# Q tails as rows of two tokens, x of two batches turned by DMA, turned q of one batch on VectorE, the last tile in halves, and a new order of every engine: a change to a scheduled attention-and-mixer kernel

## The chip, the cores, the metric

One core of one Trainium2 chip. The metric is device time in microseconds (us) of one execution. The kernel before took 213.88 us (median of six runs: five of 213.44 to 215.09 and one outlier of 687.24, its first execution). Engines: PE is TensorE (matmul), PEld its weight load, DVE is VectorE, ACT is ScalarE, POOL is GpSimd, SP is SyncE, whose only work here is to issue DMA transfers. PSUM is the memory that TensorE writes its results to.

## The reference

```
kv  = einsum('bhsd,bhse->bhde', k, v)            # 8 batches, 8 heads, 576 tokens, 64 wide
x   = einsum('bhsd,bhde->bhse', q, kv)           # then divided by its rms, times g_norm
x   = x, heads side by side                      # [8, 576, 512]
th  = x @ w_theta
y   = w_tok_r @ (x*cos(th)) + w_tok_i @ (x*sin(th))   # mixes tokens, 576 x 576
u   = x + y
out = u + relu(u @ w_ch)
```

576 tokens are four tiles of 128 and a tail of 64. Everything on TensorE is in f16 but the k/v product (f32).

## The kernel before

The kernel holds a list scheduler of its own. A function lists some 1,200 operations with engine, estimated duration, dependences and buffers; a greedy pass places each on its engine by tables of priorities (found by an earlier search) and emits each engine's instructions in that order. **Each engine then runs its list strictly in order**: an instruction that waits holds up everything behind it on its engine. The plan also gives a start time for each operation, so a trace can be compared with it; "late by 3 us" below means 3 us after the planned start. (The plan is the kernel's own estimate, no time of the chip.)

The parts that matter, cut (a cut is marked `# ...`):

```python
CAPS = {"raw": 3, "raw0": 1, "th": 5, ...}   # PSUM banks by use; raw0: products of batch 0's pairs

def load_ql(b):                              # the q tail: 64 tokens on 64 partitions, 256 B pieces
    nc.sync.dma_start(out=live["qls", b][0:T], in_=q[b, :, SF:S, :].rearrange("h s d -> s h d"))

def cast_ql(b, r):                           # two casts of 64 partitions
    (nc.gpsimd if b else nc.vector).tensor_copy(live["qcs", b][0:T, NF]..., live["qls", b][0:T]...)

def turn_x(b, ti):                           # x -> xT on TensorE, four 128x128 turns
    px = ps(("px", b, 10 + ti), [P, NK, P], FP16)
    for kc in range(NK):
        turn(px[:, kc, :], live["xs", b, ti][:, kc * P:(kc + 1) * P], kc == 0, kc == NK - 1)

def turn_x_out(b, ti):                       # and out of PSUM by ScalarE, times g_norm
    nc.scalar.activation(out=live["xTs", b][:, :, cols], in_=px..., func=AFT.Copy, scale=gcol[:])

def move_q(b, ti): ...                       # transposing DMA of turned q, on nc.sync
def move_u(b, kc): ...                       # transposing DMA of turned u (batches 1 to 6), on nc.sync
# ...
for o in todo:                               # emit in the plan's order
    take(o)
    run[o.key[0]](*o.key[1:])
in_traced_order(tc)                          # each engine keeps that order
```

So SyncE's queue carries the loads of k, v, q, the stores, the transposing transfers of q of batches 2 to 7 ("qm") and of u of batches 1 to 6 ("um").

Of the kernel before, what the change touches and what calls it, by code (L numbers as in the profile page):

```python
# [16 lines left out]
NT = NF + 1  # L17
# [7 lines left out]
    "raw": 3, "raw0": 1, "th": 5, "y": 4, "tp": 4, "vp": 2, "kvp": 4, "ya": 2, "pw": 2,  # L25
# [5 lines left out]
    "y": (85.98, 4.64), "ch": (70.71, 3.55), ("ld", 0): (-551.558, 24.603),  # L31
    ("ldq", 0): (-84.801, 30.972), ("ldwn", 0): (-44.649, 7.382), ("wth", 0): (-30.466, 14.156),
    ("gc", 0): (-297.6, 0.42), "qlk": (77.128, 26.338), ("qlk", 0): (125.519, 15.962),
    ("trig", 0): (-78.347, 5.13), "qk": (-34.53, 2.38), ("qk", 0): (-209.879, 41.386),
    ("qT", 0): (124.511, 7.245), ("kv", 0): (-314.985, 21.611), ("raw", 0): (-56.358, 23.768),
    ("sq", 0): (-297.663, 7.254), ("red", 0): (-64.845, 24.252), ("x", 0): (22.546, 7.894),
    ("xT", 0): (-258.984, 7.246), ("warm", 0): (0.0, 0.0), ("ql", 0): (-95.0, 0.0),
    ("th", 0): (-158.553, 19.296), ("y", 0): (-19.59, 31.172), ("ch", 0): (-83.183, 11.874),
    ("wT", 0): (43.363, 14.579), ("y", 1): (162.463, 15.976), ("th", 7): (40.799, 6.691),
    ("qT", 6): (92.566, 2.306), ("kv", 1): (7.371, 7.022), ("th", 1): (-97.635, 3.004),  # L40
    ("xT", 7): (-146.054, 10.265), ("kv", 6): (-44.874, 4.461), ("qT", 2): (-51.393, 29.586),
    ("y", 6): (158.768, 18.411), ("th", 2): (96.726, 5.301), ("kv", 2): (-256.637, 0.243),
    ("ch", 7): (14.444, 17.739), ("qT", 1): (371.632, 34.698), ("xT", 1): (-178.409, 10.514),
    ("raw", 2): (-95.52, 5.553), ("ch", 1): (-34.723, 1.72), ("y", 2): (241.06, 31.996),
    ("xT", 2): (-168.828, 29.651), ("raw", 1): (-119.672, 4.715), ("raw", 7): (-281.754, 42.731),
    ("th", 6): (-361.807, 1.907), ("raw", 6): (90.115, 11.6), ("kv", 7): (65.543, 8.625),
    ("y", 7): (53.63, 11.856), ("xT", 6): (131.303, 14.225), ("qT", 7): (82.373, 11.581),
    ("ch", 2): (30.558, 8.156), ("ch", 6): (-63.776, 17.286), ("qm", 0): (-4.55, 1.87),
    ("qk", 1): (85.079, 5.691), ("qm", 1): (-4.55, 1.87), ("ldq", 1): (-37.749, 1.246),
    ("ld", 1): (239.462, 7.156), ("qk", 2): (-70.196, 8.941), ("qm", 2): (17.143, 8.098),  # L50
    ("ldq", 2): (-141.334, 55.7), ("ld", 2): (-27.317, 33.594), ("qT", 3): (107.543, 43.615),
    ("kv", 3): (-17.488, 20.747), ("raw", 3): (-80.403, 13.527), ("xT", 3): (30.225, 23.067),
    ("th", 3): (77.995, 21.672), ("y", 3): (97.277, 4.882), ("ch", 3): (202.822, 0.27),
    ("qk", 3): (-153.759, 30.169), ("qm", 3): (-22.075, 1.419), ("ldq", 3): (-275.782, 13.975),
    ("ld", 3): (216.514, 24.119), ("qT", 4): (28.346, 27.685), ("kv", 4): (90.651, 20.35),
    ("raw", 4): (-153.533, 22.737), ("xT", 4): (-62.726, 1.455), ("th", 4): (3.657, 11.924),
    ("y", 4): (24.904, 15.117), ("ch", 4): (198.106, 24.141), ("qk", 4): (40.856, 8.572),
    ("qm", 4): (23.964, 16.153), ("ldq", 4): (-88.434, 3.571), ("ld", 4): (43.679, 24.455),
    ("qT", 5): (-34.135, 2.34), ("kv", 5): (1.555, 21.749), ("raw", 5): (-123.597, 27.191),
    ("xT", 5): (-30.413, 6.665), ("th", 5): (121.909, 4.616), ("y", 5): (241.657, 26.751),  # L60
    ("ch", 5): (-34.508, 3.995), ("qk", 5): (-86.719, 16.349), ("qm", 5): (-57.086, 2.954),
    ("ldq", 5): (145.527, 0.406), ("ld", 5): (227.208, 14.205), ("qk", 6): (321.876, 10.214),
    ("qm", 6): (70.998, 5.698), ("ldq", 6): (-253.55, 21.874), ("ld", 6): (121.226, 13.583),
    ("qk", 7): (19.015, 18.584), ("qm", 7): (31.956, 10.06), ("ldq", 7): (71.348, 13.703),
    ("ld", 7): (-528.83, 7.976),
}
BASE = [101.396, -104.418, 20.511, 23.351, 96.224, -0.653, -131.991, 221.778]
SWITCH = 121.22
NUDGE = {
    ("qk", 0, 0, 0): 45.66, ("qk", 0, 0, 1): -35.14, ("qk", 0, 1, 1): 3.31, ("qlk", 0, 0): -87.51,  # L70
    ("qlk", 0, 1): -31.69, ("qT", 0, 0): 1.14, ("qTc", 0, 0): -454.88, ("qT", 0, 1): -0.97,
    ("qTc", 0, 1): -440.89, ("qT", 0, 2): -409.52, ("qTc", 0, 2): 3.53, ("qT", 0, 3): -0.88,
    ("qTc", 0, 3): -384.0, ("qT", 0, 4): -2.47, ("qTc", 0, 4): -3.06, ("kv", 0, 0): -196.13,
    ("kvc", 0, 0, 0): 7.48, ("kvc", 0, 0, 1): 7.14, ("kv", 0, 1): 420.66, ("kvc", 0, 1, 0): 13.07,
    ("kvc", 0, 1, 1): 13.17, ("kv", 0, 2): 7.99, ("kvc", 0, 2, 0): -28.12, ("kvc", 0, 2, 1): 30.0,
    ("kv", 0, 3): -26.28, ("kvc", 0, 3, 0): -0.98, ("kvc", 0, 3, 1): -0.88,
    ("raw", 0, "p0"): -212.39, ("sq", 0, "p0"): -2.16, ("red", 0, "p0"): 96.15,
    ("rc", 0, "p0"): -1.39, ("x", 0, "p0"): -91.01, ("raw", 0, "p1"): -203.57,
    ("sq", 0, "p1"): 6.7, ("red", 0, "p1"): 73.67, ("rs", 0, "p1"): 104.92,
    ("rc", 0, "p1"): -45.43, ("x", 0, "p1"): -0.83, ("raw", 0, "p2"): 15.66,  # L80
    ("red", 0, "p2"): 1.03, ("x", 0, "p2"): -8.62, ("raw", 0, "p3"): -299.44,
    ("sq", 0, "p3"): 19.1, ("red", 0, "p3"): 20.09, ("rs", 0, "p3"): 20.81,
    ("rc", 0, "p3"): -15.67, ("x", 0, "p3"): -62.02, ("raw", 0, 4): -10.64, ("sq", 0, 4): -10.67,
    ("red", 0, 4): -11.52, ("eps", 0, 4): -60.36, ("pow", 0, 4): -33.3, ("x", 0, 4): -227.04,
    ("xTp", 0, 0): -14.84, ("xTpc", 0, 0): -45.82, ("xTp", 0, 1): -3.95, ("xTpc", 0, 1): -59.57,
    ("xTp", 0, 2): 232.38, ("xTpc", 0, 2): -55.33, ("xTp", 0, 3): -18.33, ("xTpc", 0, 3): -51.34,
    ("xTc", 0, 4): 109.62, ("th", 0, 0): -61.6, ("pt", 0, 0): -100.1, ("f", 0, 0): -17.58,
    ("fa", 0, 0): 28.08, ("sn", 0, 0, 0): -160.53, ("cs", 0, 0, 0): 6.58, ("th", 0, 1): 7.72,
    ("pt", 0, 1): -113.42, ("f", 0, 1): 7.34, ("fa", 0, 1): 9.17, ("sn", 0, 1, 0): -1.81,
    ("cs", 0, 1, 0): -0.97, ("z", 0, 1): -18.6, ("th", 0, 2): 17.35, ("pt", 0, 2): -132.82,  # L90
    ("f", 0, 2): -9.58, ("fa", 0, 2): -34.38, ("sn", 0, 2, 0): 8.03, ("cs", 0, 2, 0): 13.21,
    ("z", 0, 2): 11.52, ("th", 0, 3): -51.01, ("pt", 0, 3): -200.07, ("f", 0, 3): 2.32,
    ("fa", 0, 3): 1.7, ("sn", 0, 3, 0): -219.2, ("cs", 0, 3, 0): -1.01, ("z", 0, 3): 2.32,
    ("th", 0, 4): 118.68, ("pt", 0, 4): -7.5, ("f", 0, 4): -203.17, ("fa", 0, 4): -96.52,
    ("sn", 0, 4, 0): -4.26, ("sn", 0, 4, 1): -2.73, ("cs", 0, 4, 0): -308.3,
    ("cs", 0, 4, 1): -0.23, ("z", 0, 4): -234.81, ("yo", 0, 0): 81.77, ("yo", 0, 1): 115.23,
    ("yo", 0, 2): 112.8, ("yo", 0, 3): -282.63, ("yo", 0, 4): -457.22, ("yo", 0, 5): 11.54,
    ("yo", 0, 6): 158.34, ("uo", 0, 0): -274.01, ("uo", 0, 1): 41.98, ("y", 0, 4): 98.69,
    ("uy", 0, 4): -437.57, ("uy", 0, 5): -388.26, ("y", 0, 6): -3.94, ("uy", 0, 6): -167.62,
    ("y", 0, 7): -10.0, ("uy", 0, 7): -478.36, ("ut", 0, 0): -185.49, ("u", 0, 0): -276.36,  # L100
    ("ch", 0, 0): 3.37, ("o", 0, 0): 0.71, ("st", 0, 0): 235.98, ("ut", 0, 1): 228.83,
    ("u", 0, 1): -2.14, ("ch", 0, 1): 50.82, ("o", 0, 1): 39.28, ("st", 0, 1): 39.98,
    ("ut", 0, 2): -147.96, ("u", 0, 2): -0.14, ("ch", 0, 2): -90.28, ("o", 0, 2): 6.69,
    ("st", 0, 2): 3.57, ("ut", 0, 3): 37.51, ("u", 0, 3): -208.65, ("ch", 0, 3): -239.79,
    ("o", 0, 3): 79.47, ("st", 0, 3): 329.71, ("qk", 1, 0, 0): 128.3, ("qk", 1, 0, 1): 105.41,
    ("qk", 1, 1, 0): 100.2, ("qk", 1, 1, 1): 76.9, ("qlk", 1, 1): -9.45, ("qT", 1, 0): -134.25,
    ("qTc", 1, 0): -11.97, ("qT", 1, 1): -49.4, ("qTc", 1, 1): -525.43, ("qTc", 1, 2): -557.61,
    ("qT", 1, 3): 15.72, ("qTc", 1, 3): 27.23, ("qT", 1, 4): -0.81, ("kv", 1, 0): -23.38,
    ("kv", 1, 1): 12.97, ("kvc", 1, 0): 18.6, ("kvc", 1, 1): 255.16, ("kvc", 1, 2): 1.73,
# [255 lines left out]
def work(want):  # L365
# [208 lines left out]
    for i in range(2):  # L574
        add(("ldwl", i), "POOL", 600, at("ldwn", 0, i), load=450)
# [753 lines left out]
```

## Time and profile before

| | before |
|---|---|
| time, median (us) | 213.88 |
| span of the profiled run (us), mean granted TensorE clock | 211.0, 0.992 |
| busy: TensorE, ScalarE, VectorE, GpSimd (us) | 194.5, 156.2, 157.8, 103.3 |
| TensorE work at full clock, from instruction counts (us) | 178.1 |
| transposing transfers on SyncE, mean issue (us) | 48, 1.35 |

### The profile page before, as it was taken

What the parts mean: (1) busy time and instruction counts of PE and PEld (TensorE: products, weight loads), DVE (VectorE), ACT (ScalarE), POOL (GpSimd) and SP (SyncE); (2) the same over time, 40 slices, a digit from 0 to 9 for tenths busy, and PEclk for the clock granted to TensorE, in tenths of its full rate; (3) what the DMA queues carried; (4) which work ended last, traced back from release to release, by engine and by line L of the source; (5) the groups of instructions that cost most, each with busy time, mean ns of one, the idle gap of its engine ahead of it and who ended that gap; (6) DMA issues with size and microseconds to landing.
All of it is one profiled execution on the core that took longest, in us unless ns stands there. A gap on an engine that the chain in (4) does not pass through costs nothing.

```text
span 211.0 us, 6358 instructions
## 1 busy us (share of the span) xinstructions
PE 194.5 (92%) x2555; PEld 134.6 (64%) x2555; DVE 157.8 (75%) x287; ACT 156.2 (74%) x328; POOL 103.3 (49%) x141
## 2 busy tenths in 40 slices
PE   6784998899999997999799999999999999999992
PEld 1662468665778673687577576776656876667661
DVE  3266398698779859968878669969998399894572
ACT  2465999879975799999659796999896838970301
POOL 1008753799729647863693449608950098000000
PEclk9999699999999999999999999999999999999999
DMA  6999999995999999999997998779996502645154
GB/s 206 370 336 281 364 186 212 292 383 145 258 186 253 215 290 247 352 267 227 343 150 170 319 365 124 202 114 318 370 206 138 185 3 51 94 160 147 71 204 176
DMA packets 54993, 47.36 MB, mean 224 GB/s; under 512 B 32564, under 2 KB 41396, under 8 KB 54964
## 3 DMA queue, kind: packets, MB, share of 16 engines
q1 hardware_dynamic: 53988, 45.10, 84.2%
q0 software_dynamic: 976, 1.85, 5.2%
q8 instruction: 20, 0.33, 0.6%
q14 instruction: 9, 0.07, 0.2%
HBM read 33.06 MB, written 9.44 MB: 201 GB/s over the span
## 4 chain that ended last, share of the span: by engine, by line
PE 66%; ACT 15%; DMA 11%; DVE 4%; SPq 1%; issue 1%; POOL 1%; DVEq 0%
PE ys L863 28%; PE ths L863 13%; PE vps L863 12%; ACT trs L1176 6%; DMA qfs<-in_q_dram 5%; PE px L866 4%; PE kvx L863 3%; DMA wst<-in_moe_w_theta_dram 3%; DMA kvs<-in_v_dram 3%; ACT pts L1144 2%; PE rw L863 2%; ACT fas L1158 2%; ACT sqs L1059 2%; PE kvy L863 2%; PE pus L866 1%; ACT bd L1040 1%
## 5 line engine op out<-in xcount | busy, mean ns | idle before, releaser
L863 PE MATMUL ys<-wT,zs 128*128 128x320 f16 (+1 forms) x540 | 74.2, 287 | 0.0
L863 PEld LDWEIGHTS <-zs 128*128 128x128 f16 x576 | 55.0, 98 | 17.0 <-issue 1.1
L1076 POOL TENSOR_TENSOR rt<-ss,mhalf 128x8 f32<-128x8 f32 x36 | 60.4, 1680 | 2.9
L863 PE MATMUL ths<-wth,xTs 128*128 128x512 f16 (+1 forms) x192 | 38.3, 354 | 0.0
L863 PE MATMUL vps<-wch,uTs 128*128 128x512 f16 x144 | 36.2, 379 | 0.2
L1224 DVE SCALAR_TENSOR_TENSOR uTs<-ys,gcol,xTs 128x320 f16<-128x320 f32 (+1 forms) x60 | 30.1, 513 | 6.9 <-PE ys L863 6.8
L1064 DVE TENSOR_REDUCE ss<-sqs 128x8 f32<-128x512 f32 x36 | 23.7, 678 | 10.4 <-ACT sqs L1059 10.2
L1150 DVE SCALAR_TENSOR_TENSOR fs<-pts,ths 128x512 f32<-128x512 f32 (+1 forms) x40 | 25.0, 628 | 8.0 <-ACT pts L1144 7.9
L1176 ACT ACTIVATE trs<-fs 128x512 f16<-128x512 f32 (+1 forms) x48 | 26.5, 556 | 1.1 <-DVE fs L1150 0.8
L1071 POOL TENSOR_SCALAR ss<-ss 128x8 f32<-128x8 f32 x36 | 9.2, 256 | 35.9 <-DVE ss L1064 33.6
L1176 ACT ACTIVATE trs<-fas 128x512 f16<-128x512 f32 (+1 forms) x48 | 26.4, 558 | 0.3
L1144 ACT ACTIVATE pts<-ths 128x512 f32<-128x512 f32 (+1 forms) x40 | 22.1, 553 | 5.8 <-PE ths L863 5.6
L1059 ACT ACTIVATE sqs<-rw 128x512 f32<-128x512 f32 x36 | 20.5, 595 | 7.8 <-PE rw L863 7.7
L1125 ACT ACTIVATE xTs<-px,gcol 128x512 f16<-128x512 f16 (+1 forms) x36 | 22.7, 638 | 4.4 <-PE px L866 4.3
L1098 DVE TENSOR_TENSOR xs<-rw,rt 128x512 f16<-128x512 f32 x36 | 24.6, 683 | 1.2 <-POOL rt L1076 0.9
L863 PEld LDWEIGHTS kvx<-kvs,kvs 64*64 64x64 f32 x576 | 20.6, 135 | 6.2 <-issue 4.1
L863 PE MATMUL kvx<-kvs,kvs 64*64 64x64 f32 x576 | 22.8, 221 | 1.7 <-DMA kvs<-in_v_dram 1.3
L897 POOL CAST qc<-qfs 128x512 f16<-128x512 f32 x28 | 17.6, 653 | 13.1 <-DMA qfs<-in_q_dram 13.0
L863 PEld LDWEIGHTS <-xTs 128*128 128x128 f16 (+1 forms) x192 | 15.1, 103 | 13.7 <-issue 1.9
L863 PE MATMUL kvy<-kvs,kvs 64*64 64x64 f32 x576 | 22.4, 221 | 0.0
L1158 ACT ACTIVATE fas<-fs 128x512 f32<-128x512 f32 (+1 forms) x35 | 20.2, 585 | 2.0 <-DVE fs L1150 1.9
L1185 DVE TENSOR_TENSOR zs<-xs,trs 128x1024 f16<-128x1024 f16 x28 | 19.7, 707 | 1.8 <-ACT trs L1176 1.4
(72 smaller groups left out, 223.6 us busy)
## 6 DMA issues: line engine op xcount, KB each, us to landing
kvs<-in_k_dram SPq DMA_DIRECT2D x32, 288.0 KB, 6.2
kvs<-in_v_dram SPq DMA_DIRECT2D x32, 288.0 KB, 6.1
out_dram<-ots SPq DMA_DIRECT2D x32, 256.0 KB, 2.8
qfs<-in_q_dram SPq DMA_DIRECT2D x14, 512.0 KB, 7.8
qfs<-in_q_dram SPq DMA_DIRECT2D x4, 256.0 KB, 5.4
wst<-in_moe_w_theta_dram SPq DMA_DIRECT2D x2, 512.0 KB, 6.3
qls<-in_q_dram SPq DMA_DIRECT2D x8, 128.0 KB, 7.1
out_dram<-ots SPq DMA_DIRECT2D x8, 128.0 KB, 3.4
```

What stands on the lines that cost most here:

```text
L863: nc.tensor.matmul(dst, lhsT, rhs, start=first, stop=last)
L1059: nc.scalar.activation(out=live["sqs", b, ti][:], in_=live["rw", b, ti][:], func=AFT.Square)
L1064: nc.vector.reduce_sum(out=ss[:], in_=live["sqs", b, ti][:].rearrange("p (h e) -> p h e", h=H), axis=mybir.AxisListType.X,)
L1076: nc.gpsimd.tensor_tensor(out=rt[:], in0=st["ss", b, ti][:], in1=mhalf[:], op=ALU.pow)
L1098: nc.vector.tensor_tensor(out=x.rearrange("p j (h e) -> p j h e", e=D), in0=live["rw", b, ti][:].rearrange("p (j h e) -> p j h e", j=n, e= ...
L1125: nc.scalar.activation(out=live["xTs", b][:, :, cols], in_=live["px", b, 10 + ti][:, :, 0:cols.stop - cols.start], func=AFT.Copy, scale=gc ...
L1144: nc.scalar.activation(out=live["pts", b, ti][:, 0:n], in_=live["ths", b, ti][:], func=AFT.Identity, bias=MAGIC)
L1150: nc.vector.scalar_tensor_tensor(out=live["fs", b, ti][:, 0:n], in0=live["pts", b, ti][:, 0:n], scalar=MAGIC, in1=live["ths", b, ti][:], o ...
L1158: nc.scalar.activation(out=live["fas", b, ti][:, 0:n], in_=live["fs", b, ti][:, 0:n], func=AFT.Abs)
L1176: nc.scalar.activation(out=dst, in_=src, func=AFT.Sin, scale=-RAD, bias=math.pi / 2 if cos else 0.0)
L1185: nc.vector.tensor_tensor(out=z[:], in0=x.unsqueeze(1).broadcast_to((P, 2, C)), in1=tr[:], op=ALU.mult)
L1224: nc.vector.scalar_tensor_tensor(out=live["uTs", b // 2][:, kc, pair_cols(b, cols)], in0=live["ys", b, i][:], scalar=gcol[:], in1=live["xT ...
```

## The change

Its intent: TensorE, the bound, loses the turns of x of batches 6 and 7; ScalarE, full in 20 to 40 us, loses copies; the tail loads move in bigger pieces; the last store starts earlier. All tables of priorities and caps were searched anew, so the order of every engine is new. The core of the diff (tables and repeated lines cut):

```diff
-    "raw": 3, "raw0": 1, "th": 5, "y": 4, "tp": 4, "vp": 2, "kvp": 4, "ya": 2, "pw": 2,
+    "raw": 3, "raw0": 3, "th": 4, "y": 4, "tp": 5, "vp": 2, "kvp": 4, "ya": 6, "pw": 3,
# WANT, BASE, SWITCH, NUDGE: all new (cut)
-SPARED = (2, 3)
+SPARED = (2,)
+CARRIED = (6, 7)
+LAST = (7, 3)
 def load_ql(b):
-    nc.sync.dma_start(out=live["qls", b][0:T], in_=q[b, :, SF:S, :].rearrange("h s d -> s h d"))
+    nc.sync.dma_start(
+        out=live["qls", b].rearrange("p h j d -> p h (j d)"),
+        in_=q[b, :, SF:S, :].rearrange("h (p j) d -> p h (j d)", j=2),
+    )
# cast_ql: four casts of 32 partitions, all on GpSimd; the mixer's tail rows to match (cut)
 def turn_q_out(b, hp):
-        nc.scalar.copy(out=t, in_=pq)
+        if b == 1:
+            nc.vector.tensor_copy(t, pq)
+        else:
+            nc.scalar.copy(out=t, in_=pq)
+    def move_x(b, ti):                       # batches 6 and 7, tiles 0 to 3
+        nc.sync.dma_start(
+            out=live["xTs", b][:, :, tokens(b, ti)], in_=live["xs", b, ti][:], transpose=True
+        )
+    def scale_x(b, ti):
+        xT = live["xTs", b][:, :, tokens(b, ti)]
+        nc.vector.tensor_scalar(out=xT, in0=xT, scalar1=gcol[:], scalar2=None, op0=ALU.mult)
# channel, channel_out, store: tile (7, 3) in two halves of 256 columns (cut)
 def store(b, ti):                            # output tails of a pair of batches
-            for r in range(2):
-                nc.sync.dma_start(out=out[b - 1 + r, SF:S, :], in_=ot[r * T:(r + 1) * T, :])
+            for r in range(4):
+                dst = out[b - 1 + r // 2, SF:S, :].rearrange("(p j) c -> j p c", j=2)
+                nc.sync.dma_start(out=dst[r % 2], in_=ot[r * TH:(r + 1) * TH, :])
# mixer_out: ScalarE for three of nine, VectorE for six (before: five and four) (cut)
```

## The prediction

> **What bounds the kernel now.** I read the page first (busy shares, the 40 slices), then the chain of waits, then the table of windows, then the timeline of the parts that the change touches.
>
> ```profile
> PE 194.5 (92%) x2555; PEld 134.6 (64%) x2555; DVE 157.8 (75%) x287; ACT 156.2 (74%) x328; POOL 103.3 (49%) x141
> ...
> PE   6784998899999997999799999999999999999992
> ...
> DMA  6999999995999999999997998779996502645154
> ...
> PE 66%; ACT 15%; DMA 11%; DVE 4%; SPq 1%; issue 1%; POOL 1%; DVEq 0%
> ```
>
> TensorE is at 92%, and from about 42 us (slice 8) to 205 us it is hardly ever idle. So in the middle only less TensorE work, or the removal of a few short holes, can shorten the run. The whole idle time is 211.0 − 194.5 = 16.5 us, and the windows say where it lies:
>
> ```profile
> core 0: us, PE busy (x) PEld busy (x) DVE busy (x) ACT busy (x) POOL busy (x), PEclk, DMA share, GB/s
> 10.00:20.00 10.00, 6.80 (x115) 4.85 (x114) 6.89 (x16) 6.40 (x18) 3.22 (x3) 1.00 1.11 305
> 20.00:30.00 10.00, 8.48 (x127) 4.74 (x131) 5.54 (x11) 9.33 (x19) 8.17 (x14) 0.83 1.05 299
> 30.00:40.00 10.00, 8.28 (x169) 7.44 (x160) 8.32 (x17) 9.79 (x23) 3.84 (x10) 1.00 1.12 219
> ...
> 100.00:110.00 10.00, 8.70 (x134) 6.51 (x133) 7.72 (x14) 6.75 (x13) 7.49 (x8) 1.00 1.26 258
> 160.00:188.00 28.00, 28.00 (x356) 19.65 (x354) 22.04 (x41) 21.23 (x45) 9.52 (x10) 1.00 0.41 95
> ```
>
> Idle TensorE: 2.8 us before 10 us, 3.2 us in 10 to 20, 1.5 in 20 to 30 (and there the granted clock was 0.83), 1.7 in 30 to 40, some 3.5 us in all in the holes at 80 to 90, 100 to 110 and 120 to 130, and 3.8 us at the very end; that is the 16.5. In 20 to 40 us ScalarE is the full one: 19.1 of 20 us. Behind the hole at 100 to 110 stands a k/v load (the wait list has TensorE waiting 1.3 us for it) while the DMA share is above 1. From 160 to 188 us TensorE has no gap at all and the DMA share is only 0.41.
>
> The start has one serial chain of its own. Batch 0 goes by head pairs, and the plan gives their raw products a single PSUM bank (the cap "raw0": 1):
>
> ```profile
> 12.15 0.69 DVE L1098 TENSOR_TENSOR x<-rw_p,rt_p 128x512 f16<-128x512 f32 x1
> ...
> 12.62 0.40 PE L863 MATMUL rw_p<-bd,qTs 128*128 128x128 f16 x4
> ...
> 15.84 0.69 DVE L1098 TENSOR_TENSOR x<-rw_p,rt_p 128x512 f16<-128x512 f32 x1
> ...
> 18.74 0.69 DVE L1098 TENSOR_TENSOR x<-rw_p,rt_p 128x512 f16<-128x512 f32 x1
> 18.82 0.39 PE L863 MATMUL rw_p<-bd,qTs 128*128 128x128 f16 x4
> ...
> 23.66 2.93 PE L863 MATMUL ths<-wth,xTs 128*128 128x512 f16 x6
> ```
>
> The last pair's raw product (18.82) starts only as the pair before is being scaled out of the bank (18.74), although its k/v matmuls had ended at about 14.5. Then reduce, root, scale (21.41), turn (22.19): theta begins at 23.66.
>
> **What the Trainium skill says.** "DMA: Bandwidth & Descriptors", Specifications, wants pieces of at least 512 B for line rate and says that smaller ones are read-modify-written. The trace neither proves nor refutes the threshold; what it has is that a tail load of 128 KB takes 7.1 us to land, about as long as a q load of 512 KB (7.8). "Advanced Engine Details and Errata", X-Bar Transpose (TRN2), calls transposing DMAs as fast as plain ones, 350 to 400 GB/s. The trace does not agree for tiles of this size: one takes 1.26 us of the sync queue, so 128 KB per 1.26 us is at most 104 GB/s, and lands 2.4 (least) to 4.3 us (median) after issue. "Perfetto Trace Analysis", Optimizing Scalar/DVE Operations, says that where VectorE has a faster mode it beats ScalarE, unless it is saturated; the trace agrees: the copies of turned mixer weights take 633 ns on ScalarE and 447 ns on VectorE. The same page, Matmuls, wants independent groups to rotate through PSUM banks so that emptying one overlaps the next; the chain above is the opposite, by plan.
>
> **The change part by part.**
>
> *q tails.* 8 loads of 512 pieces of 256 B become 8 loads of 256 pieces of 512 B: 2,048 packets fewer of 53,988. I put the gain in DMA time at under 1 us per load, most of it hidden. Four casts over 32 partitions replace two over 64. If a cast costs by its columns, each is still about 0.39 us (median of the 14 on GpSimd), so GpSimd gets 14 × 0.39 + 4 × 0.39 (batch 0, from VectorE) = +7.0 us, less one theta cast (1.56) = +5.4: 103 to about 109 us, 52%. Not a bound, but GpSimd also holds the 1.68 us power in each tile's chain. Tail stores and the mixer's tail load double their number of DMAs: 8 stores more, about 0.55 us of the sync queue each.
>
> *x of batches 6 and 7 by DMA.* Eight sets of four turns leave TensorE. Four turns cost 0.22 us in the chain (44.43 to 44.65), so 8 × 0.22 = 1.8 us, and those of batch 7 lie in the stretch where it has no gap. ScalarE loses 8 × 0.68 = 5.4 us; VectorE gains 8 in-place scalings, for which I estimate 0.25 us each (f16 in SBUF, below the 0.42 of the f32 cast of the same size) = 2.0 us. But the path from x to xT gets longer: 0.4 + 0.7 us becomes 1.26 (issue) + 1.2 to 3 (flight) + 0.25. For batch 7 the DMA is idle, so nearer the short end. For batch 6 (145 to 156 us) it is not: the sync queue there is full of transposes and stores:
>
> ```profile
> 147.19 1.23 SPq L1242 DMA_TRANSPOSE ums<-uTs  x1
> 148.85 0.81 SPq L1263 DMA_DIRECT2D out_dram<-ots  x2
> 149.72 5.33 SPq L1242 DMA_TRANSPOSE ums<-uTs  x3
> 155.15 1.72 SPq L1263 DMA_DIRECT2D out_dram<-ots  x2
> 156.97 5.14 SPq L1002 DMA_TRANSPOSE qTs<-qc  x4
> ```
>
> Four more add 5 us to it ahead of the transposes of batch 7's q. I count 1.8 us gained and 0.5 lost: −1.3.
>
> *ScalarE to VectorE.* Turned q of batch 1: 5 copies of 0.584 leave ScalarE (−2.9), about 0.41 each on VectorE (+2.1, scaled from 0.447 for 576 columns). Mixer copies: five on ScalarE become three (−1.3), four on VectorE become six (+0.9). Together 4.2 us leave ScalarE in the 20 to 40 us where it is full, and VectorE has 4.5 and 1.7 us free in the two halves.
>
> *The start.* "raw0" goes from 1 bank to 3, "ya" and "pw" get more, and the fourth theta cast leaves GpSimd (1.56 us, it ended at 19.9) for VectorE (0.42). The last pair need not wait about 3.5 us for its bank, so theta may begin near 20 instead of 23.7. Not all of it arrives: loads run at 282 to 305 GB/s with a DMA share near or above 1, and batch 1's q landed at 21.7. Of the 6.4 us idle in 10 to 40 I expect 2.5 back (−2.5).
>
> *The last tile in halves.* It ends with 0.88 us of matmuls, 0.69 on VectorE and a store. The second half's VectorE part is about 0.42 (−0.27), its store half as big (say −0.1): −0.4.
>
> *The middle.* Fewer packets and a newly searched order may take a little of the 3.5 us of holes: −0.6. The order is new everywhere, so this is the least certain term.
>
> Totals: ScalarE 156 − 9.6 = 147; VectorE 158 + 2.1 + 2.0 + 0.9 + 0.4 (theta cast) − 1.0 (tail casts of batch 0) + 0.2 (halves) = 162; TensorE 194.5 − 8 × 0.39 (the records of four turns overlap what follows) = 191. Time: −1.3 − 2.5 − 0.4 − 0.6 = −4.8 us.
>
> From what? The three runs were 687.24, 215.09 and 213.44, the profiled one 212.77. The first is an outlier, and the median is in truth the slower of two good runs; I start from 214.0. 214.0 − 4.8 = 209.2.
>
> **The rivals.** (a) *The longer x path of batch 7 takes the gain back.* The last-batch products wait for its last modulated tile (188.55 + 0.41) and start at 188.33: TensorE's filler and that chain end together now. Three us more in the chain would open a hole there, unless the channel tiles held back until after 195 us fill it. For it: the full sync queue at 147 to 162. Against: the first k/v product of batch 7 runs at 162.5 and there are 26 us to move things in. Time about 212.5. (b) *The start is bound by loads.* For it: DMA share 1.11, 1.05, 1.12, and TensorE waiting for casts of batch 1's q. Then the freed bank and ScalarE time only move the idle time, and 1 us comes back, not 2.5: about 211. (c) *The new order closes the holes too*, and a denser start keeps the clock at 1.00 in 20 to 30 us (16 theta matmuls took 5.16 us there; four sets at the 0.86 us of the last batches would be 3.44): up to 3 us more, about 206.5. (d) *GpSimd or VectorE becomes the bound*: 52% and 77% speak against it, save in stretches such as 150 to 160 us where VectorE is already 100% busy.
>
> **Range and chances.** (a) and (b) together give about 213, (c) 206; I take 205.5 to 213. Faster by 2% means below about 209.7; my centre lies just under it, and the rivals on the slow side are a little heavier: faster 0.52, same 0.45, slower 0.03.
>
> **What would show each step.** Theta of batch 0 starting near 20 us and TensorE busy over 17.5 of the 20 us in 20 to 40: the start. Raw products of the pairs less than 2 us apart: the bank. The turns of x down by 32 in count, and no gap in 160 to 188: the x part. A VectorE wait for a transposing DMA, or a TensorE gap at 165 to 190, would be rival (a). Tail loads landing well under 7 us: the q tails. A last VectorE piece of about 0.42 us: the halves. The sum is wrong if the middle, which I read least, gains or loses more than 2 us by its new order.

## More of the kernel before

The prediction shows most of the page. Two views are added here because the result turns on them: the table of windows for two later stages of the kernel before (columns: window, length, busy us of PE, PEld, DVE, ACT, POOL, each with its count of instructions, then granted clock, mean DMA share, GB/s),

```profile
85.00:90.00 5.00, 4.89 (x98) 3.20 (x96) 4.54 (x10) 4.73 (x9) 4.21 (x7) 1.00 1.03 351
90.00:95.00 5.00, 5.00 (x63) 4.21 (x64) 3.29 (x7) 5.00 (x11) 3.04 (x3) 1.00 1.25 262
...
150.00:160.00 10.00, 10.00 (x73) 6.28 (x71) 10.00 (x19) 9.97 (x20) 6.03 (x9) 1.00 1.19 246
```

and the tail load's row of the DMA issues (KB each, median us from issue to landing):

```profile
qls<-in_q_dram SPq DMA_DIRECT2D x8, 128.0 KB, 7.1
```

TensorE has almost no gap in these windows and the clock is full.

## The result

217.31 us (median of six, 216.81 to 218.15) against 213.88: a ratio of 1.016 (1.012 to 1.020). A ratio is the mean time of one kernel's fast runs over that of the other's of the same rounds, so not quite the ratio of the medians quoted, which are of all its runs. The change is 3.4 us slower where I had expected 4.8 us faster, and it lies outside my range; at the 2% level it counts as the same. The profiled run was the slowest of the six (218.15, span 216.4, clock 0.975).

The page of the changed kernel: busy times, the slices of TensorE and of its clock (40 slices of 5.4 us), and the chain by engine:

```profile
PE 197.0 (91%) x2527; PEld 134.4 (62%) x2527; DVE 161.9 (75%) x302; ACT 149.3 (69%) x313; POOL 111.0 (51%) x160
...
PE   6981895999999997699999999999999899999993
...
PEclk9999589999999999799999999999999999999999
...
PE 45%; ACT 19%; DVE 10%; DMA 10%; POOL 6%; issue 4%; SPq 3%; DVEq 0%; POOLq 0%
```

28 matmul instructions are gone (32 turns less, 4 more for the halves). ScalarE fell by 6.9 us (9.6 had been worked out) and GpSimd rose by 7.7 (5.4 had been). TensorE's busy time rose by 2.5 us. The clock slices, counted from 0, show where matmuls take longer: 5 in slice 4 (22 to 27 us) and 7 in slice 16 (87 to 92 us). TensorE's share of the chain fell from 66% to 45%: more of the end is waits. The windows of the changed kernel (from two tables):

```profile
20.00:30.00 10.00, 8.04 (x104) 4.53 (x104) 5.04 (x12) 5.67 (x10) 8.98 (x18) 0.66 0.96 307
30.00:40.00 10.00, 7.47 (x158) 5.60 (x151) 9.35 (x19) 8.61 (x20) 6.24 (x10) 1.00 1.04 246
...
85.00:90.00 5.00, 2.71 (x67) 1.94 (x60) 4.30 (x8) 5.00 (x11) 2.88 (x5) 0.96 1.44 325
90.00:95.00 5.00, 5.00 (x89) 2.83 (x88) 3.43 (x7) 3.81 (x9) 4.70 (x5) 0.70 0.95 257
...
150.00:160.00 10.00, 9.87 (x185) 5.95 (x175) 8.50 (x18) 9.07 (x23) 0.55 (x1) 1.00 0.58 109
```

Three stages stand out: the start, 85 to 95 us, and 150 us onwards. **At the start**, VectorE's timeline (start us, us busy, engine, line, operation, in brackets the idle time before it and what ended it):

```profile
17.10 0.76 DVE L958 TENSOR_SCALAR wth<-wst 128x512 f16<-128x512 f32 x2 [3.26 <-DMA wst<-in_moe_w_theta_dram]
...
19.16 0.43 DVE L958 TENSOR_SCALAR wth<-wst 128x512 f16<-128x512 f32 x1 [0.70 <-DMA wst<-in_moe_w_theta_dram]
```

The theta weights landed at 17.08 and 19.14 us (14.84 and 16.70 in the kernel before, though issued 0.35 us later there). VectorE stood at their casts, with the sums of the last two pairs behind them in its list, and TensorE stood in turn. (The cast at 19.16 is the one that the change moved from GpSimd.) In the kernel before, VectorE had only the two casts of the first half and stood 0.4 us for them (a row of its table of lines: busy us, mean ns, idle us before and what ended it):

```profile
L928 DVE TENSOR_SCALAR wth<-wst 128x512 f16<-128x512 f32 x2 | 0.8, 422 | 0.4 <-DMA wst<-in_moe_w_theta_dram 0.4
```

TensorE's timeline in the changed kernel, at the start and in the middle:

```profile
21.15 0.46 PE L890 MATMUL px<-ident,x 128*128 128x128 f16 x4 [4.50 <-DVE x L1139]
...
87.11 0.40 PE L890 MATMUL px<-ident,xs 128*128 128x128 f16 x4 [0.95 <-DVE xs L1139]
...
89.03 0.40 PE L890 MATMUL px<-ident,xs 128*128 128x128 f16 x4 [1.30 <-DVE xs L1139]
...
91.05 1.91 PE L887 MATMUL ths<-wth,xTs 128*128 128x512 f16 x4
```

In windows of 1 us the granted clock is 0.50 from 22 to 28 us, behind the gap of 4.50 us, and again from 90 to 93, behind the pair of gaps (between the two it was still 1.00). Four theta matmuls, from the first start to the last end, take 1.91 us at 91 us and 1.03 us where the clock is full (at 141 us). **From 139 to 157 us** the lines of SyncE and two of VectorE:

```profile
142.82 1.20 SPq L1165 DMA_TRANSPOSE xTs<-xs  x1
144.12 3.83 SPq L1040 DMA_TRANSPOSE qTs<-qc  x3
147.99 1.26 SPq L1292 DMA_TRANSPOSE ums<-uTs  x1
149.38 4.62 SPq L1165 DMA_TRANSPOSE xTs<-xs  x3
...
145.50 0.68 DVE L1139 TENSOR_TENSOR xs<-rw,rt 128x512 f16<-128x512 f32 x1
156.99 0.35 DVE L1171 TENSOR_SCALAR xTs<-xTs,gcol 128x512 f16<-128x512 f16 x1 [1.02 <-DMA xTs<-xs]
```

Tile 3 of x of batch 6 is written at 145.50 + 0.68 = 146.2; its transfer, the last of the three in the group at 149.38, is issued at 152.73, since SyncE issues one transposing transfer after another without a pause. It is scaled at 156.99, and theta of that tile follows at 157.40. In this profile TensorE itself stood there for only about 0.1 us. Batch 7's tiles, in contrast, are issued within 0.14 us of being written. The tail loads, for comparison with 7.1:

```profile
tails<-in_q_dram SPq DMA_DIRECT2D x8, 128.0 KB, 6.7
```

**A ledger of TensorE's time.** I took each TensorE operation of a trace, gave it its length at full clock (0.22 us for four turns or a raw product, 0.86 for theta or channel, 1.05 for k/v, and so on), and called the rest of the time up to the next operation lost, whatever it was: waits, half clock, dummy matmuls. By stage (us):

| profile | work | 0-40 | 40-70 | 70-100 | 100-144 | 144-end |
|---|---|---|---|---|---|---|
| before | 178.1 | 19.3 | 1.2 | 4.1 | 3.5 | 0.8 |
| before, second profile | 178.1 | 20.0 | 2.3 | 3.6 | 2.9 | 0.8 |
| after | 176.4 | 22.6 | 1.6 | 7.4 | 2.3 | 2.5 |

The work fell by 1.7 us, as predicted. The losses rose by 3 us at the start, 3.5 in 70 to 100 and 1.7 in the last stage.

### The profile page after: what moved, and what is told of

It reads as the page before. It is cut to its first block, busy times and chain, and to the rows that moved or that the text cites. A ratio compares the mean times of both kernels' runs of the same rounds, so it can differ in the third digit from the quotient of the medians.

```text
span 216.4 us, 6348 instructions
## 1 busy us (share of the span) xinstructions
PE 197.0 (91%) x2527; PEld 134.4 (62%) x2527; DVE 161.9 (75%) x302; ACT 149.3 (69%) x313; POOL 111.0 (51%) x160
## 3 DMA queue, kind: packets, MB, share of 16 engines
q1 hardware_dynamic: 56564, 46.15, 82.3%
## 4 chain that ended last, share of the span: by engine, by line
PE 45%; ACT 19%; DVE 10%; DMA 10%; POOL 6%; issue 4%; SPq 3%; DVEq 0%; POOLq 0%
PE ys L887 17%; PE ths L887 10%; PE vps L887 8%; ACT trs L1226 7%; POOL rt L1117 5%; DMA wst<-in_moe_w_theta_dram 4%; ACT sqs L1100 3%; PE kvx L887 3%; ACT pts L1194 2%; DMA qfs<-in_q_dram 2%; ACT fas L1208 2%; DVE ss L1105 2%; ACT xTs L1175 2%; DMA xTs<-xs 2%; PE px L890 2%
## 5 line engine op out<-in xcount | busy, mean ns | idle before, releaser
L887 PE MATMUL ys<-wT,zs 128*128 128x320 f16 (+1 forms) x540 | 72.7, 287 | 0.0
L887 PE MATMUL ths<-wth,xTs 128*128 128x512 f16 (+1 forms) x192 | 40.6, 366 | 0.4
L887 PE MATMUL vps<-wch,uTs 128*128 128x512 f16 (+1 forms) x148 | 35.5, 374 | 0.0
L1208 ACT ACTIVATE fas<-fs 128x512 f32<-128x512 f32 (+1 forms) x35 | 20.6, 587 | 5.3 <-DVE fs L1200 5.2
L887 PEld LDWEIGHTS kvx<-kvs,kvs 64*64 64x64 f32 x576 | 21.1, 138 | 4.8 <-issue 3.4
L887 PE MATMUL kvy<-kvs,kvs 64*64 64x64 f32 x576 | 23.3, 224 | 0.8 <-DVE uTs L1274 0.8
L887 PE MATMUL kvx<-kvs,kvs 64*64 64x64 f32 x576 | 23.5, 224 | 0.1
L1235 DVE TENSOR_TENSOR zs<-xs,trs 128x1024 f16<-128x1024 f16 x28 | 20.3, 729 | 2.8 <-ACT trs L1226 2.7
L887 PEld LDWEIGHTS kvy<-kvs,kvs 64*64 64x64 f32 x576 | 21.1, 138 | 0.9 <-DVE uTs L1274 0.9
L887 PEld LDWEIGHTS <-uTs 128*128 128x128 f16 x148 | 13.7, 98 | 12.1 <-issue 0.6
```

The source lines that it names most:

```text
L887: nc.tensor.matmul(dst, lhsT, rhs, start=first, stop=last)
L1208: nc.scalar.activation(out=live["fas", b, ti][:, 0:n], in_=live["fs", b, ti][:, 0:n], func=AFT.Abs)
L1235: nc.vector.tensor_tensor(out=z[:], in0=x.unsqueeze(1).broadcast_to((P, 2, C)), in1=tr[:], op=ALU.mult)
```

## The experiments

Eighteen runs were made. Those built on the changed kernel keep its order on every engine but for what the edit names, since only the emission is edited, not the plan. Ten ledgers and how late TensorE was against its plan, for use below. Each ratio is to the kernel before in the same rounds; two changed kernels are compared through these ratios unless they ran in the same rounds.

| run | time (us) | ratio to before | 0-40 | 70-100 | 100-144 | 144-end | late at 144 | late at 176 |
|---|---|---|---|---|---|---|---|---|
| the change | 217.31 | 1.016 | 22.6 | 7.4 | 2.3 | 2.5 | 10.3 | 11.8 |
| tails_old | 216.62 | 1.013 | 21.2 | 7.1 | 2.6 | 3.7 | 9.2 | 11.9 |
| norm_early | 218.86 | 1.024 | 20.8 | 7.1 | 2.1 | 5.4 | 8.3 | 12.7 |
| warm_more | 215.86 | 1.010 | 20.1 | 7.1 | 2.6 | 2.9 | 8.1 | 10.1 |
| x6_first | 220.24 | 1.034 | 19.5 | 6.5 | 2.0 | 7.6 | 6.3 | 12.9 |
| um2_early | 218.36 | 1.020 | 21.1 | 5.7 | 3.3 | 4.3 | 8.5 | 11.8 |
| no_um23 (wrong result) | 215.75 | 1.010 | 20.3 | 7.2 | 2.1 | 1.7 | 7.9 | 8.8 |
| sp_order | 215.56 | 1.004 | 20.4 | 7.0 | 2.2 | 1.9 | 8.0 | 9.0 |
| sp_order_again | 215.68 | 1.010 | 20.6 | 7.2 | 2.1 | 1.9 | 8.2 | 9.2 |
| sp_fill | 214.45 | 1.004 | 19.8 | 6.1 | 2.3 | 2.0 | 7.0 | 8.1 |

(The profile is one run of each; the start differs from run to run by up to 2 us.)

### The start: what holds the theta weights back?

**tails_old** puts the layout of the tails back in the changed kernel's order.

```diff
-    out=live["qls", b].rearrange("p h j d -> p h (j d)"), in_=q[...].rearrange("h (p j) d -> p h (j d)", j=2)
+    out=live["qls", b][0:T], in_=q[b, :, SF:S, :].rearrange("h s d -> s h d")
# casts 0 and 1 as before, 2 and 3 empty; mixer rows and output tails as before
```

> The changed kernel with only the layout of the tails put back (q tails loaded on 64 partitions in pieces of 256 B, two casts of 64 partitions, output tails stored as before); every engine keeps the changed order, two of four casts are gone. Theory A: the new shape of the tail loads, issued right behind the theta weights, holds those weights back. Then theta's two loads land near 14.8 and 16.7 us again as in the kernel before (17.1 and 19.1 in the changed one), VectorE's wait of 3.3 us at theta's cast and TensorE's gap of 4.5 us at 16.7-21.2 go, theta starts near 20.6, and the time falls by 4 to 5 us to 212-213.5. Theory B: the loads are late for another reason (their place behind the small g_norm loads, or the transfers ahead of them); then they land near 17 and 19 again and the time stays at 216-217.5, at most 0.7 less for the casts saved.

216.62 us (ratio 1.013), and the weights landed at 15.66 and 18.04. Theory A falls: the shape of the tail loads is not what holds them back.

**norm_early** issues the two small g_norm loads from ScalarE's queue before anything else.

```diff
-            nc.sync.dma_start(out=gcol[r * D:(r + 1) * D, :], in_=g_norm.unsqueeze(1))
+            nc.scalar.dma_start(out=gcol[r * D:(r + 1) * D, :], in_=g_norm.unsqueeze(1))
# and called once ahead of the loop
```

> The changed kernel with the two small g_norm loads issued by ScalarE's queue before anything else, in place of by SyncE right ahead of theta's loads. Theory B: the hole in the DMA engines at 11.4-12.8 us, where the 4-byte packets of g_norm lie, is what delays theta. Then the theta weights land near 14.5 and 16 us, and the time falls by 4 to 5 us to 212-213.5. Theory A (the tail loads behind theta do it): theta lands near 16.5 and 18.5, only the earlier issue gained, and the time stays at 216-217.5.

218.86 us, slower; the weights landed at 16.30 and 18.06. Theory B falls too, though the test is not clean: the theta loads were issued at 9.99 here, 1.3 us later than in the change. From issue to landing the first took 6.3 us, and 6.4 in warm_more (below), which leaves the g_norm loads in their place. Over all profiles of changed kernels the first half landed between 14.88 and 17.08, so the profile of the change was an extreme one and chance has a part. But the run's windows showed something new: the start was better (loss 20.8) and the time worse, for a hole had opened where the change had none:

```profile
140.00:150.00 10.00, 8.63 (x119) 5.59 (x121) 8.39 (x16) 7.81 (x16) 7.05 (x7) 1.00 0.78 136
150.00:160.00 10.00, 8.52 (x146) 4.75 (x136) 7.08 (x15) 7.55 (x20) 0.12 (x1) 1.00 0.63 83
```

**warm_more** puts 20 dummy matmuls into TensorE's gap.

```diff
+        if o.key == ("warm", 13):
+            for n in range(14, 34):
+                warm(n)
```

> The changed kernel with 20 more dummy matmuls of 0.22 us behind the last warming one, so that TensorE has no gap at 16.7-21 us. Theory C: 2.3 us of the late start is the halved TensorE clock behind that gap (theta's first three groups took 1.9 us each and not 0.9). Then the clock is near 0.97 or above in 20-30 us (0.66 in the changed kernel), batch 1's first kv group begins 2 us earlier, at about 27, and the time falls by 1.5 to 2.5 us to 215-216. Rival: behind theta the stage is held by VectorE and ScalarE anyway; then the clock is kept but the time stays at 216.5-217.5.

215.86 us (1.010); the clock was 1.00 in 20 to 30 us. The medians say that filling the gap gains 1.4 us, as theory C expected; by the ratios (1.005 to 1.015 against 1.012 to 1.020) it is not clear of noise.

### Is it the parts, or the order?

**three_parts** puts the tails, the copies of q of batch 1 and the halves into the order of the kernel before; **tails_only** the tails alone. (x by DMA can't be tried so: that order leaves 2.5 to 3.5 us between x and its theta.)

```diff
# before's cast_ql(b, r), same engine and place in the order:
-    tensor_copy(live["qcs", b][0:T, NF]..., live["qls", b][0:T]...)
+    for j in range(2):
+        tensor_copy(live["qcs", b][j * TH:(j + 1) * TH, NF]..., live["qls", b]...[:, :, r:4:2, j, :])
# both: loads, the mixer's tail rows and output tails to match (cut)
# three_parts also: nc.vector.tensor_copy for b == 1; matmuls, sum and store of tile (7, 3) in halves (cut)
```

> The kernel before with three of the four parts put into its own order unchanged: q tails as rows of two tokens (with two casts in place of each one), turned q of batch 1 copied by VectorE, the last tile in two halves. If the parts are good and the new order is what costs, the time is 213-214.3, no worse than the kernel before (213.9). Rival (Theory A, the tail loads' shape costs wherever they stand): theta's loads land at 17 and 19 us here too and the time is 216 or more.

> The kernel before with the q tails as rows of two tokens alone (two casts of 32 partitions for each cast of 64, loads, mixers' rows and output tails to match), its order unchanged. With three parts on the old order the time was 215.7 against 214.1. If the tails are what cost (twice the casts: on VectorE in the start, some 0.6 us, and 3 us more on GpSimd over the rest): 215.3-216. If it is the copies of q of batch 1 on VectorE or the halves: 213.7-214.5.

215.71 (1.009) and 215.80 (1.013). The tails alone make the old order slower, and the other two parts together bring nothing that shows. In the profile with the tails alone, theta of batch 0 starts at 25.55 us (23.66 and 24.69 in the two of before), with four casts of batch 0's tail on VectorE in the middle of the serial start. More of it lies in the tail casts of the later batches, which are on GpSimd in both kernels. TensorE's waits for them, in the kernel before and then with the tails alone (us in total, times, longest):

```profile
PE pq L866 <- POOL qc L900: 0.2, 1, 0.2
...
PE pq L868 <- POOL qc L906: 3.5, 3, 1.5
```

Two of these three waits, 0.85 and 1.48 us, fall in 80 to 100 us. Ahead of the second, four casts took GpSimd 2.50 us, where two took 0.74 in the kernel before. So the price, in this one profile, is that of the doubled casts. In the profiles of the change and of sp_order TensorE has no wait for a tail cast, and the layout costs nothing that shows (tails_old above, and tails_sp below).

**before_again**, a second profile of the kernel before, unchanged:

> The kernel before, unchanged, for a second profile. If the late landing of the theta weights (15.7 to 17.1 us in five profiles with changes, 14.8 in the one profile of before) comes of chance in the transfers, it lands at 15.5-17 here too; if it comes of the change, at 14.6-15.2. Time 213.5-215.

213.46 us, the first weights at 14.78: in both profiles of the kernel before, they landed earlier than in all of the changed ones, if only by 0.04 us against the earliest. Why stays open.

### Does SyncE's queue set the end?

Theory D, formed from norm_early: its x of batch 6, tile 2, was written at 142.3 and issued at 152.5. The column "late at 144" against "late at 176" says the same: starts that were up to 4 us better came to nothing by 176 us.

**x6_first** issues x of batch 6 as soon as each tile is written, ahead of the q transfers.

```diff
+    behind(("xm", 6, 2), ("x", 6, 2)); behind(("xm", 6, 3), ("x", 6, 3)); behind(("xm", 6, 1), ("x", 6, 1))
# behind(a, b): emit a right after b, so that only SyncE's order changes
```

> The changed kernel with the transposing transfers of x of batch 6 issued by SyncE as soon as each x is written, ahead of those of turned u of batch 3 and turned q of batch 7 that stood before them. Theory D: in 136-166 us SyncE issues without a pause (1.2 us for each transposing transfer), so x of batch 6, tile 3, ready at 146.2, was issued at 152.7 only, and theta of that tile waited for it. Then that transfer is issued near 148, theta of tiles 1 and 3 of batch 6 starts 2 to 4 us earlier, TensorE's holes in 150-170 (about 1.3 us in all) close, and the time falls by 1 to 1.7 us to 215.5-216.3. Rival: those holes are slack and what comes later (z of batch 6, y of batch 6) does not wait for them; then the time stays within 0.5 of 217.3.

220.24 us: much worse, a miss for the cure. Tile 3 went out at 146.6 as wanted, but tile 1, whose theta is the first of the two in TensorE's list, was now behind tile 3, two of q and one of u: written at 143.5, issued at 149.9, landed at 154.0. TensorE's timeline:

```profile
154.47 2.88 PE L896 MATMUL ths<-wth,xTs 128*128 128x512 f16 x12 [3.65 <-DVE xTs L1180]
```

A gap of 3.65 us, and half clock behind it. TensorE, only 6.3 us late at 144, was 12.9 late at 176. The wait for the queue is the cost that theory D names, but my cure put the wrong tile last: the queue is too full for one tile to pass without another falling back.

**no_um23** takes eight transfers out of the queue. Its output is wrong, which doesn't matter for the time.

```diff
     def move_u(b, kc):
+        if b in (2, 3):
+            return
# the output sum of batches 2 and 3 reads the unturned u
```

> Wrong result on purpose: the changed kernel without the eight transposing transfers of u of batches 2 and 3 (the output sum of these two batches reads the unturned u, so their output is wrong); nothing else moves. It takes some 10 us of issues out of SyncE's queue between 130 and 160 us, and no work from any other engine. Theory D (SyncE's queue sets the end since x of batches 6 and 7 goes through it): x of batch 6 is then sent within 1 us of being written, the holes of TensorE in 144-176 us close, and the time falls by 1.5 to 3 us to 214.3-215.8. Rival (the late start sets the end and SyncE only follows): at most 0.5 less, 216.8-217.5.

215.75 us (1.010). Tiles 0 and 1 of batch 6 were issued within 0.1 us of being written (2.4 and 1.9 in the change); tiles 2 and 3 still waited 4.5 and 3.9 us (6.3 and 6.5). TensorE was full:

```profile
150.00:160.00 10.00, 10.00 (x72) 6.13 (x71) 7.90 (x16) 9.69 (x24) 0.00 (x0) 1.00 0.48 143
```

It lost 1.7 us after 144 and grew only 0.9 us later by 176.

**um2_early** and **um2_warm** move four of these transfers to 112 us instead, correct.

```diff
+    for kc in range(NK):
+        behind(("um", 2, kc), (("uy", 2, 7), ("um", 2, 0), ("um", 2, 1), ("um", 2, 2))[kc])
# um2_warm: and the 20 dummy matmuls
```

> The changed kernel, correct, with the four transposing transfers of u of batch 2 issued near 112-117 us, where SyncE stands waiting for free buffers and u is complete since 114, in place of 130-160. Theory D: SyncE's queue is some 5 us shorter when x of batch 6 is ready, and the time falls by 0.8 to 2 us to 215.3-216.5. Rival (late start sets the end): 216.8-217.8. Against it: the k and v loads of batch 6 behind them are issued up to 5 us later; if these then come too late the time rises.

> Both cures in the changed kernel: u of batch 2 turned early and 20 dummy matmuls in the gap of the start. If the late start (clock, worth 1.4 us in the run with dummy matmuls alone) and SyncE's queue are two separate costs, the gains add: 213.5-214.8, level with the kernel before. If SyncE's queue takes back what the start gains, the two together give more than the sum of the two alone, 213 or less. If neither cure of the queue works: 215.5-216.2, as with the dummy matmuls alone.

218.36 and 217.96: both missed. The four took 7.4 us there (112.0 to 119.4, 1.5 to 2.2 us each), the loads of batch 6 and all behind them slipped, and the queue arrived at x of batch 6 just as late: issued at 143.4 with the tile written at 138.9. The waits of SyncE in 112 to 119 were not the free time that I took them for, or not enough of it.

**sp_order** changes the order alone in 130 to 158 us: what is needed late goes behind x of batch 6.

```diff
+    for (key, last) in (
+        (("um", 3, 3), ("um", 3, 2)), (("xm", 6, 2), ("x", 6, 2)), (("xm", 6, 3), ("x", 6, 3)),
+        (("xm", 6, 1), ("x", 6, 1)), (("st", 3, 4), ("xm", 6, 1)), (("um", 2, 0), ("qm", 7, 0)),
+        (("um", 2, 1), ("um", 2, 0)),
+    ):
+        behind(key, last)
# sp_order_warm: and the 20 dummy matmuls; sp_order_again: the same file
```

> The changed kernel, correct, with SyncE's order alone changed in 130-158 us: two transfers of u of batch 2 and the tail store of batches 2 and 3 (4.7 us of issues) go behind the four transfers of x of batch 6, and these are issued in the order in which x is written. No transfer is dropped. Theory D (SyncE's queue holds x of batch 6 back): the last of the four is issued near 148 and not 153, TensorE's lateness against its plan grows by less than 1 us from 144 to 176 us (1.7 to 4.4 in the others), and the time is 215.3-216.3. Rival (fewer transfers helped, not the order): 216.8-218, as with the other two reorderings.

> A repeat of sp_order with more rounds. If SyncE's order is worth what it showed, 215-216 and a ratio of 1.003 to 1.010 to the kernel before; if the first result was luck (one of its four runs was 212.7), 216.5 or more.

> The same order of SyncE and in addition 20 dummy matmuls in the gap of the start. Theory D with the late start as a separate cost: the gain of the start (1.5 us) is no longer taken back in 144-176 us, and the time is 213.8-214.8, level with the kernel before. Rival: 215.5-216.2, as with the dummy matmuls alone.

sp_order: 215.56 us (212.74 to 216.04, the highest a slow run; ratio 1.004, 0.997 to 1.011, from three fast runs); the repeat 215.68 (1.010, 1.006 to 1.015). SyncE's timeline in sp_order:

```profile
142.02 1.19 SPq L1177 DMA_TRANSPOSE xTs<-xs  x1
...
145.93 2.52 SPq L1177 DMA_TRANSPOSE xTs<-xs  x2
148.50 2.90 SPq L1339 DMA_DIRECT2D out_dram<-ots  x4
```

All four of x are issued by 147.24, at most 2.1 us after being written, and the tail store (2.9 us) comes behind them. TensorE grows 1.0 us later from 144 to 176 (1.5 in the change). Every transfer is still there, and the time is that of no_um23, which dropped eight: so the order of the queue does it and not the traffic. How much it is worth is less sure. The change and the repeat ran in different rounds and their intervals touch (1.012 to 1.020, 1.006 to 1.015). A second pair points the same way: tails_sp (below) is this order with the old tails, and has 1.008 against the 1.013 of tails_old. The dummies on top did not add their gain: sp_order_warm took 216.33 (1.011). Its profile shows two candidates, neither tested alone. The 20 dummies ran on to 20.94 us and held back a turn whose x was ready at 19.19. And TensorE stood for 1.0 us in the k/v product of batch 7, where the profile names no engine that it waited for ("issue"); all three kernels with 20 dummies at the start and nothing else new on TensorE have such a stall of 1.0 to 1.3 us, and the change itself and sp_order have none.

**tails_sp** undoes the tails on top of that order.

> The changed kernel with SyncE's order changed as in the run before, and in addition the layout of the tails put back. If the tails cost through SyncE's queue (stores of output tails 2 to 3 us against 1.15 us) and GpSimd's extra casts, as 0.7 us alone and more once SyncE's order no longer hides it: 214.3-215.2, x of batch 6 sent at once. Rival (the tails are neutral): 215.3-216.

215.61 us (1.008), level with sp_order: the rival holds, and the tails are neutral in the changed order.

### The holes at 85 to 90 us

Over the profiles of the changed order in which the granted clock stayed at 1.00 in 85 to 95 us, the loss in 70 to 100 us is 5.6 to 6.5 us; in those where it dropped, 7.0 to 7.4.

**warm_both** fills the holes by 38 dummy turns, on top of the dummies at the start; **tails_sp_mid** does so on top of tails_sp.

```diff
+        for n in range({(3, 0): 16, (3, 2): 22}.get((b, ti), 0)):
+            turn(px[:, n % NK, :], ident[:], n % NK == 0, n % NK == NK - 1)
```

> The changed kernel with the 20 dummy matmuls at the start, and in addition 16 and 22 dummy turns of 0.056 us in TensorE's two holes at 86-89 us (ahead of the turns of x of batch 3, tiles 0 and 2). Theory C for the middle: the halved clock behind those holes (mean 0.85 in 90-100 us; theta of batch 3 took 1.55 and 1.91 us and not 0.86) costs 1.5 us. Then the clock is near 1.0 in 80-100 us and the time is 1 to 1.5 us under that with the start alone (215.9), at 214.4-215. Rival: ScalarE (9.9 of 10 us busy in 80-90) sets that stage; then the clock is kept and the time stays at 215.5-216.2.

> As the run before, with 16 and 22 dummy turns of 0.056 us ahead of the turns of x of batch 3, tiles 0 and 2, so that TensorE's holes at 85-89 us are filled. If the clock behind these holes costs 1.5 us: the clock in 85-95 us is at 1.0 and the time is 1 to 1.8 us below that run, 213-213.8, a little under the kernel before. Against it: [...] a stall of 3 us at the kv product of batch 6 spoilt the earlier run with these turns, and may appear again elsewhere. Rival (the clock is not on the path): no change, 214.3-215.2.

218.82 (1.026) and 216.14 (1.010): no gain over warm_more (1.010) and tails_sp (1.008). The clock was kept (1.00), but in warm_both TensorE stood for 3.1 us at 130 us in the k/v product of batch 6, again with no engine named. That these stalls come of the extra instructions is a guess from when they appear; no run shows their cause. The profile of tails_sp_mid is of a slow run, and nothing is read from it.

**sp_fill** uses ten long dummy matmuls in place of 38 turns, on top of sp_order.

```diff
+        for n in range({(3, 0): 4, (3, 2): 6}.get((b, ti), 0)):
+            dot(fill[:], zero[:, 0:P], zero, True, True)     # the bank that px takes next
```

> SyncE's order changed as before (run sp_order), and 4 and 6 dummy matmuls of 0.22 us ahead of the turns of x of batch 3, tiles 0 and 2, so that TensorE's holes at 85-89 us are filled with 20 instructions in place of 76. If the halved clock behind these holes costs the time 1.5 us: clock 1.0 in 85-95 us, TensorE's loss in 70-100 us (without the dummies counted as work) down from 7.1 to 5.6, time 1 to 1.8 us under the repeat of sp_order, near 214. Rival (off the path, or taken back later as with the start): level with it within 0.5.

214.45 us (213.93 to 215.50), 1.2 us under sp_order_again in the same rounds (ratio of the means 0.994; by the spread of the six runs of each, 0.3 to 2.2 us). The windows of sp_order_again and then of sp_fill:

```profile
85.00:90.00 5.00, 3.71 (x22) 2.12 (x23) 3.84 (x7) 4.57 (x10) 2.80 (x6) 0.69 1.26 215
90.00:95.00 5.00, 5.00 (x104) 3.77 (x102) 3.48 (x6) 4.26 (x10) 4.72 (x8) 0.97 1.19 292
...
85.00:90.00 5.00, 4.89 (x75) 2.84 (x77) 3.95 (x8) 4.89 (x10) 2.85 (x5) 1.00 1.25 238
90.00:95.00 5.00, 5.00 (x82) 3.96 (x72) 4.29 (x9) 4.90 (x13) 4.78 (x8) 1.00 1.26 200
```

No useful work was added or removed: the holes are as long, but filled, and the granted clock behind them is full. So the half clock costs about 1.2 us of the time, and a timed pair shows it. The gaps do not always bring it: um2_early has the same two (0.94 and 1.30 us), and its clock stayed at 1.00 in 85 to 95 us.

**sp_fill_warm** adds 12 dummies at the start.

> The run sp_fill with 12 more dummy matmuls in the gap of the start, which end near 19.3 us and so do not hold the turn of x of pair 2 back (20 ended near 20.9). If the start's clock is a separate cost: clock above 0.95 in 20-30 us, 0.7 to 1.5 us under sp_fill, 212.8-213.8, level with the kernel before or a little under. Rival (taken back later, or the 24 instructions move a stall of the instruction stream): 214.2-215.5.

215.50 us (1.008): the rival holds. The clock was 1.00 in 20 to 30 us and nothing came of it at the end (late by 8.6 us at 176, against 8.1), and here no stall without a named engine is there to blame. But the theta weights landed at 16.78 us in this profile and at 14.88 in that of sp_fill, so the two starts do not compare one to one. The gain at the start, 1.4 us by the medians and not clear of noise, did not show on top of the other two cures.

No version beat the kernel before. The best, sp_fill, is 0.4% behind it (1.0041, 1.0004 to 1.0078).

## Why the prediction was wrong, step by step

Against the kernel before, the ledger of the change's profile gives: work −1.7, start +2.9 (22.6 against the mean of 19.3 and 20.0), 40 to 70 −0.2, 70 to 100 +3.5 (7.4 against 3.9), 100 to 144 −0.9, last stage +1.7: +5.3 in all, of a profiled run that was 0.8 us above the median.

**x by DMA, "1.8 us gained and 0.5 lost".** The gain is there: the work at full clock fell by 1.7. The step that failed is the loss, which was mis-sized. I had seen that SyncE's queue was full around 150 us and counted "5 us ... ahead of the transposes of batch 7's q", but I charged TensorE 0.5 for it. The changed kernel sends x itself through that in-order queue, and tile 3 of batch 6 was issued 6.5 us after being written, behind what is needed later. The loss after 144 us was 1.7 us more than before in the change's profile, up to 4.6 more in others whose start was better. In the change's profile TensorE's direct waits for x by DMA are short, 0.1 us each for batches 6 and 7, and its one gap of size there, 0.58 us before 169.54, is for a u that VectorE wrote late; so "no gap in 160 to 188" failed too. Where the start was better the wait came out: two gaps of 1.37 and 1.48 us in norm_early. The cost in time is 1.2 to 1.8 us by order alone, as far as sp_order shows it (1.8 by the medians, 1.2 by the repeat's ratio; the intervals touch). Rival (a) named the mechanism, the longer x path, but the wrong batch: batch 7's x was issued on time, batch 6's was not.

**The start, −2.5.** The bank step was right: the last two raw products moved from 18.82 and 15.22 to 14.34 and 14.97, 0.63 us apart. But theta of batch 0 began at 23.86 in this profile and at 21.6 to 23.4 in the other changed ones, not at "near 20", and TensorE was busy 15.5 us in 20 to 40 and not 17.5. Rival (b), the start is bound by loads, was the right one: theta's weights landed at 14.9 to 17.1 us and VectorE stood at their casts with the critical sums behind them. In all sixteen profiles of the changed order theta of batch 0 began 6.3 to 7.5 us after the first weights landed. I had moved a theta cast to VectorE as pure gain and did not ask what stands behind it in that list: it waited 0.70 us for the second half of the weights. On top came the half clock (0.66 in 20 to 30), where rival (c) had expected a fuller one. The loss up to 40 us was 19.5 to 21.6 in the ten other profiles of the changed order without dummies at the start (mean 20.7, with 19.7 before), so the step is worth about +1 in place of −2.5, not the +2.9 of one profile.

**The middle, −0.6.** This is the step with the largest error: +3.5 in the profile, and over 3 in every profile of the changed order whose clock fell there. I had said that the sum was wrong if the middle moved by more than 2 us, and it did. One ground for the −0.6 was false by itself: on the queue of these transfers the packets did not become fewer but rose from 53,988 to 56,564, with eight transposing transfers more. The new order leaves two holes at 86 to 89 us, in which TensorE waits for x of batch 3; the half clock that follows costs 1.2 us of time (sp_fill). The holes themselves remain, and cost more (2.2 us of waits in the change). VectorE, which writes that x, works without a pause from 85.76 to 90.1; the first x stands in its list behind an output sum that had waited 0.70 us for a copy of ScalarE, and ScalarE was 5.00 of 5 us busy in 85 to 90. So the new order of these two engines may be the cause; that is argued only, no run tested it.

**The last tile, −0.4.** VectorE's last piece took 0.42 us, as estimated. That it saves 0.4 us was never isolated; three_parts minus tails_only shows no gain that stands out.

**q tails.** 390 ns for a cast of 32 partitions (0.39 estimated), GpSimd at 111.0 (109): near what was said. Tail loads landed at 6.7 us (7.1), not "well under 7". All of it is worth nothing that shows in the changed order, and in the old one the doubled casts cost time (tails_only, 1.013). The in-place scaling took 0.34 us and not 0.25, 0.7 us of VectorE in all. What I under-counted is the store of the output tails: four issues, 2.2 to 3.2 us of SyncE's queue each where two took 1.15.

**What stays open.** Why the theta weights land later though issued earlier (tail shape and g_norm loads are excluded, chance is part of it); whether the start's clock costs time at all (1.4 us by one pair of medians, nothing on top of the other cures); what makes the holes at 86 to 89 us; and 0.9 us of the difference that sp_fill leaves, in spite of 1.7 us less TensorE work. What is clear of noise is the sum of the two cures: the change stands at 1.016 (1.012 to 1.020) and sp_fill at 1.004 (1.000 to 1.008).

## What to carry to other kernels

When work is taken off the bound engine and given to a DMA queue, price the queue: it is an in-order engine like any other, and what a transfer waits for there is what was put ahead of it, not its own length. Here a freed 1.7 us of matmul was worth less than two idle gaps, which in most profiles were paid twice: 2.2 us as waiting, and 1.2 us as half clock behind them. And with many in-order lists a better start was kept in several runs only as far as the next full list; so check after each cure where the lateness is taken back, and time cures together before adding them up.

## What the Trainium skill lacked or had wrong

- "Advanced Engine Details and Errata", X-Bar Transpose (TRN2), says that transposing DMAs are as fast as plain ones. What binds here is the issuing, for which that page gives no time (other pages treat the cost of issuing in general): each one of 128 x 512 f16 took SyncE 1.19 us at least to issue, 1.38 on average and up to 2.63 in the change (56 transfers, 77 us of the queue), against 0.43 for a plain load of 288 KB. The 104 GB/s of the prediction is a ceiling set by this issuing, not a measured rate of the transfer. The same section wants all transposes of a core in one stream at a time, so that they can't simply be spread over two queues; no run here shows that.
- "TensorE: Matmul & The Clock Gate", HAM oscillation, puts the rule as no idle gap over some 3.4 us. The start agrees (a gap of 4.50 us, then 0.66 in 20 to 30 us). The middle is outside that rule: behind gaps of 0.95 and 1.30 us with 0.6 us of work between (2.71 of 5 us busy) the clock was halved as well, in most profiles though not in all (um2_early: the same gaps, 1.00); filling them was worth 1.2 us. The page's next section does say that frequent short pauses can bring the slow clock, but gives no length for them.
- None of the pages I read tells what such a stall is: with 20 dummy matmuls at the start, a stall of 1.0 to 1.3 us with no engine named followed some 130 us later in all three kernels, and with 38 dummy turns in addition one of 3.1 us 40 us later; ten long dummies in the same holes had no such effect.
